# Transposes by DMA, V in batches, corrected GpSimd lengths, rules by unit and 79 packs, in a planned attention and linear-attention kernel

## The chip, the cores, the metric

One core of one Trainium2 chip. The metric is device microseconds (us) of one execution; unless said otherwise a time is the median of several runs. "Span" is the time from the first to the last instruction in the profile; it is 1.7 to 3.1 us shorter than the time of the same run.

## The reference, cut

```python
x = A_x                                   # 1 x 2048 x 512, bf16; 32 heads of 16
g = sigmoid((x * gate_w).sum(-1, keepdims=True))
a = A(x)   # softmax attention: p = softmax(q k^T / 4); o = p v; o @ A_wo
b = B(x)   # linear attention: phi = [softmax(+-q w_phi)], num = phi_q (phi_k^T v), den = phi_q sum(phi_k); (num/den) @ B_wo
return g * a + (1 - g) * b
```

## The kernel before

Nearly all the work is branch A's exponentials: 32 heads of 2048 x 2048 scores. The kernel cuts them into 32 "units" (four heads by 512 queries), each of 16 key tiles by four score tiles of 128 x 512. Most score tiles go TensorE -> PSUM ring -> ScalarE (exp, in calls of three and two tiles) -> TensorE (times V). Some key tiles, the **packs**, skip ScalarE: VectorE and GpSimd build their exponentials arithmetically. Branch B's work fills gaps.

No order is written by hand. The kernel lists operations with an assumed duration, dependencies and a priority, and a **planner** in the kernel plays them through at build time, engine by engine; the order it finds is the order in which each engine gets its instructions. So the assumed durations and the constants decide the program, though no instruction contains them.

```python
PACE = [2.384, 0.458]; RULES = [...]; PIECES = (4, 4)      # constants of the planner, found by search
DVE_COUNT = (1, 3, 2, 1, 2, 3, 1, 2, ...)                  # packs per unit, 76 in all
# a pack (cut): integer scores on VectorE, then split on GpSimd (or VectorE), then a polynomial on VectorE
ws.append(s.op("dve", 0.605, lambda e: e.tensor_scalar(EW[...], self.bk(b), EC, 127 * 65536, ...)))     # x4
fs = [s.op("pool", U * 9.3e-4 + 0.03, lambda e, c=c: e.tensor_scalar(Ef[...], half(0, uint16, c, U), ...),
           alt=U / 1920 + 0.065, port=True) for c in range(US)]      # alt: may run on VectorE instead
hs = [s.op("pool", W * 9.3e-4 + 0.03, lambda e, c=c: e.tensor_scalar(ED[...], half(1, int16, c, W), ...)) ...]
u = s.op("dve", 1.13, Em = Ef * Ef); q = s.op("dve", 0.6, Em = Em * E3 + E1)
g = s.op("dve", 1.13, Em = Ef * Em); v = s.op("dve", 1.13, ED = ED + Em)
# branch B, a query tile (cut): eight transposes on TensorE into a PSUM bank, one copy on VectorE
m = s.op("pe", 0.056, lambda e: e.transpose(pb()[:, P*gg:P*gg+P], self.phi[...], self.iden[:, :]), ...)
ev = s.op("dve", 0.601, lambda e: e.tensor_copy(self.phiT[...], pb()), [m], frees=[b])
# ... and four more transposes and a copy for the result, onT_B
```

Only two PSUM banks (ps_mp) serve pack scores, projections, V, and branch B. An op marked `port` may not overlap a GpSimd op in the plan.

The softmax here doesn't subtract the row's maximum and nothing guards it: scores larger than these inputs give would overflow.

## Time and profile before

| | before |
|---|---|
| time, median of 3 (range) | 858.81 us (857.71 to 859.97) |
| span of the profiled run | 855.9 us |
| ScalarE / VectorE / GpSimd busy | 829.6 / 790.5 / 416.7 us |
| exponential calls; packs | 698; 76 |
| end by the kernel's own planner | 841.8 us |

The prediction below shows the profile's lines. In a group's line, the two numbers after the first bar are the time in which at least one such instruction ran, and the mean duration.

### The profile page before, as it was taken

The page shows a single profiled execution, that of the slowest core. Times are in us where ns is not written, and L with a number is a line of the kernel's source. Part 1 is how long each engine was busy: PE and PEld are TensorE (multiplying, and loading weights), DVE is VectorE, ACT ScalarE, POOL GpSimd, SP SyncE. Part 2 cuts the span into 40 slices and gives each one's busy share as a digit, 9 for nine tenths or more (in the row PEclk, how much of TensorE's full clock was granted, in tenths as well). Part 3 has the DMA queues.
Part 4 walks back from the last instruction along what each step waited for, and adds up shares of the span by engine and source line. Part 5 has one row for each costly group of instructions (what it writes and reads, how often), then busy time and mean ns, then how long its engine had stood idle before and what let it go on. Part 6 is the DMA issues. An engine that isn't in the chain of part 4 may idle for free.

```text
span 855.9 us, 14732 instructions
## 1 busy us (share of the span) xinstructions
PE 792.2 (93%) x5939; PEld 235.5 (28%) x5939; DVE 790.5 (92%) x1178; ACT 829.6 (97%) x770; POOL 416.7 (49%) x548
## 2 busy tenths in 40 slices
PE   8988999999999999999999899999999988898898
PEld 3222233222332223322222222222222222222222
DVE  4899998999879999899999999999999999899995
ACT  6999999999999999999999999999999999899997
POOL 1566043514024466234664754855664366745742
PEclk9999999999999999999999999999999999999999
DMA  6230100000000000000000000000000000000000
GB/s 121 56 76 4 53 4 2 2 5 4 3 2 5 4 5 4 2 4 4 8 12 10 8 17 16 4 4 1 4 5 4 4 4 4 1 4 4 5 20 31
DMA packets 23523, 11.31 MB, mean 13 GB/s; under 512 B 15904, under 2 KB 23456, under 8 KB 23456
## 3 DMA queue, kind: packets, MB, share of 16 engines
q1 hardware_dynamic: 21872, 9.99, 4.4%
q8 instruction: 46, 0.75, 0.4%
q10 hardware_dynamic: 1584, 0.39, 0.2%
q14 instruction: 21, 0.17, 0.1%
HBM read 3.69 MB, written 2.10 MB: 7 GB/s over the span
## 4 chain that ended last, share of the span: by engine, by line
ACT 44%; DVE 40%; PE 7%; POOL 6%; issue 2%; DMA 0%; SPq 0%; POOLq 0%
ACT ET L832 41%; DVE EW L917 9%; DVE Em L936 6%; DVE ED L942 5%; DVE Em L940 5%; POOL ED L931 4%; DVE Em L938 3%; PE ps_ring L815 3%; ACT phi L1086 2%; POOL Ef L927 2%; DVE Ef L927 2%; PE ps_mp L906 1%; DVE fsum L1090 1%; PE ps_ot L860 1%; DVE phi L1092 1%
## 5 line engine op out<-in xcount | busy, mean ns | idle before, releaser
L832 ACT ACTIVATE ET<-ps_ring 128x1536 bf16<-128x1536 f32 (+1 forms) x698 | 800.5, 1302 | 13.3 <-PE ps_ring L815 8.0
L815 PE MATMUL ps_ring<-qT,kT 64*128 64x512 bf16 x1744 | 349.5, 385 | 30.3 <-ACT ET L832 23.6
L927 POOL TENSOR_SCALAR Ef<-EW 128x512 f16<-128x512 uint16 x236 | 165.5, 701 | 301.2 <-DVE EW L917 83.9
L931 POOL TENSOR_SCALAR ED<-EW 128x512 int16<-128x512 int16 x304 | 248.0, 833 | 124.8 <-PE ps_ot L948 34.9
L917 DVE TENSOR_SCALAR EW<-ps_mp 128x512 int32<-128x512 f32 x304 | 196.4, 677 | 13.8 <-PE ps_mp L906 13.0
L860 PE MATMUL ps_ot<-ET,Vaug 128*17 128x512 bf16 x1744 | 169.2, 384 | 2.6 <-DVE T L977 2.3
L815 PEld LDWEIGHTS ps_ring<-qT,kT 64*128 64x128 bf16 x1744 | 73.0, 93 | 235.0 <-ACT ET L832 195.8
L906 PE MATMUL ps_mp<-qT,kT 64*128 64x512 bf16 (+1 forms) x304 | 112.3, 385 | 15.5 <-POOL ED L931 8.2
L936 DVE TENSOR_TENSOR Em<-Ef 128x2048 f16<-128x2048 f16 x76 | 97.5, 1283 | 7.5 <-POOL Ef L927 7.3
L942 DVE TENSOR_TENSOR ED<-ED,Em 128x2048 uint16<-128x2048 int16 x76 | 98.4, 1295 | 2.4 <-POOL ED L931 2.1
L940 DVE TENSOR_TENSOR Em<-Ef,Em 128x2048 f16<-128x2048 f16 x76 | 97.8, 1287 | 0.4
L877 PE MATMUL ps_ot<-zero,iden 128*32 128x512 bf16 (+2 forms) x572 | 96.5, 380 | 0.0
L860 PEld LDWEIGHTS ps_ot<-ET,Vaug 128*17 128x17 bf16 x1744 | 41.2, 87 | 140.4 <-issue 125.0
L938 DVE TENSOR_SCALAR Em<-Em 128x2048 f16<-128x2048 f16 x76 | 61.0, 803 | 0.4
L906 PEld LDWEIGHTS ps_mp<-qT,kT 64*128 64x128 bf16 (+1 forms) x304 | 28.3, 95 | 70.9 <-DVE EW L917 35.0
L1090 DVE TENSOR_REDUCE fsum<-phi 128x64 f32<-128x1024 bf16 x32 | 38.4, 1201 | 4.2 <-ACT phi L1086 4.0
L1092 DVE TENSOR_TENSOR phi<-phi,frec 128x1024 bf16<-128x1024 bf16 x32 | 40.5, 1266 | 0.2
L697 PE MATMUL ps_mp<-Wp,xT 128*128 128x512 bf16 x128 | 40.2, 384 | 0.0
L697 PE MATMUL ps_mp<-xT,WA 128*128 128x512 bf16 x128 | 38.9, 383 | 0.5 <-ACT xT L681 0.5
L1086 ACT ACTIVATE phi<-ps_mp 128x512 bf16<-128x512 f32 x64 | 37.4, 685 | 0.3 <-PE ps_mp L697 0.3
L877 PEld LDWEIGHTS ps_ot<-zero,iden 128*32 128x32 bf16 (+2 forms) x572 | 29.9, 95 | 16.8
L948 PE MATMUL ps_ot<-ED,Vaug 128*17 128x512 bf16 x304 | 29.3, 383 | 4.0 <-DVE ED L942 3.6
(86 smaller groups left out, 460.1 us busy)
## 6 DMA issues: line engine op xcount, KB each, us to landing
qT<-qst SPq DMA_DIRECT2D x120, 16.0 KB, 1.8
out_dram<-outt SPq DMA_DIRECT2D x12, 128.0 KB, 1.7
WA<-in_A_wqkv_dram SPq DMA_DIRECT2D x3, 384.0 KB, 4.5
xr<-in_A_x_dram SPq DMA_DIRECT2D x4, 128.0 KB, 3.2
WBV<-in_B_wqkv_dram SPq DMA_DIRECT2D x1, 512.0 KB, 3.9
WoA<-in_A_wo_dram SPq DMA_DIRECT2D x1, 512.0 KB, 3.8
WoB<-in_B_wo_dram SPq DMA_DIRECT2D x1, 512.0 KB, 4.5
out_dram<-outz SPq DMA_DIRECT2D x4, 128.0 KB, 1.8
```

What stands on the lines that cost most here:

```text
L815: return lambda e: e.matmul(self.ps_ring[:, x % RING, :], self.kT[r, g // 2, kt * P:(kt + 1) * P], self.qT[r, n % 2, i, :], start=True, st ...
L832: self.o_exp.append(s.op("act", w * 0.434 + 0.045, lambda e, b0=b0, s0=s0, w=w: e.activation(self.ET[:, s0:s0 + w, :], self.ps_ring[:, b0: ...
L860: return lambda e: e.matmul(self.ps_ot[32 * i:32 * i + VSL, :], self.Vaug[:, kt, h, :], self.ET[:, (4 * p + k) % NSLOT, :], start=(kt == 0 ...
L877: return lambda e: e.matmul(self.ps_ot[c:c + nc, :], self.iden[r:r + nr, 0:nc], self.zero[r:r + nr, :], start=False, stop=False, tile_posi ...
L906: return lambda e: e.matmul(self.bk(b), self.kT[r, cp, kt * P:(kt + 1) * P], self.qT[r, n % 2, i, :], start=True, stop=True, tile_position ...
L917: ws.append(s.op("dve", 0.605, lambda e, i=i, b=b: e.tensor_scalar(self.EW[:, ew.idx, i * QCH:(i + 1) * QCH], self.bk(b), float(EC), float ...
L927: fs = [s.op("pool", U * 9.3e-4 + 0.03, lambda e, c=c: e.tensor_scalar(self.Ef[:, ef.idx, U * c:U * c + U], half(0, dt.uint16, c, U), floa ...
L931: hs = [s.op("pool", W * 9.3e-4 + 0.03, lambda e, c=c: e.tensor_scalar(self.ED[:, ed.idx, W * c:W * c + W].bitcast(dt.int16), half(1, dt.i ...
L936: u = s.op("dve", 1.13, lambda e: e.tensor_tensor(self.Em[:], Ef(), Ef(), ALU.mult), fs + [self.ed_prev], pr, frees=[ef], port=True)
L938: q = s.op("dve", 0.6, lambda e: e.tensor_scalar(self.Em[:], self.Em[:], E3, E1, op0=ALU.mult, op1=ALU.add), [u], pr, port=True)
L940: g_ = s.op("dve", 1.13, lambda e: e.tensor_tensor(self.Em[:], Ef(), self.Em[:], ALU.mult), [q], pr, frees=[ef], port=True)
L942: vs = [s.op("dve", 1.13, lambda e: e.tensor_tensor(out(), out().bitcast(dt.int16), self.Em[:], ALU.add), [g_] + hs, pr, port=True)]
```

## The change

The intent: take transposes and small copies off TensorE, VectorE and the two PSUM banks; tell the planner longer GpSimd times, nearer to the measured ones; let planner rules differ by unit; and use the room for three more packs. Cut to its core:

```diff
-RULES = [1.148, 0.155, 0.715, 0.527, 2.372]      -PIECES = (4, 4)
+RULES = [0.155, 0.527, 0.1]                      +PIECES = ((2, 2), (2, 4), (4, 4))
+OFF, PRI, SHY, FILL, SLIP, POLY, SHAPE = [33 values each, one per unit] (cut)
-DVE_COUNT = (1, 3, 2, 1, 2, 3, 1, 2, 1, 1, 3, 4, ...)     # 76
+DVE_COUNT = (1, 3, 2, 2, 2, 3, 2, 2, 1, 2, 3, 3, ...)     # 79
-        fs = [s.op("pool", U * 9.3e-4 + 0.03, ...
+        fs = [s.op("pool", U * 8.26e-4 + 0.28, ...        # 512 columns: 0.51 -> 0.70 us
-        hs = [s.op("pool", W * 9.3e-4 + 0.03, ...
+        hs = [s.op("pool", W * 8.26e-4 + 0.165, ...       # 512 columns: 0.51 -> 0.59 us
-        ... 8 x e.transpose(...) on "pe", then tensor_copy to phiT on "dve"
+        ev = s.op("sp", 2.6, lambda e: e.dma_start_transpose(
+            self.phiT[:, pt.idx], self.phi[:, ph.idx].rearrange("p h s f -> p (h s f)")), [o_phi], r + 15,
+            alloc=[pt], frees=[ph], dma=1)
-        ... 4 x e.transpose(...) on "pe", then tensor_copy to onT_B on "dve"
+        self.o_onTB[t] = s.op("sp", 1.3, lambda e: e.dma_start_transpose(
+            self.onT_B[:, bt.idx], self.ob[:, ob.idx, :]), os_, r + 25, alloc=[bt], frees=[ob], dma=1)
+    def emit_V4(self, t, part):       # V of later heads: 16 matmuls for four tiles into one bank, one copy
-                    free = o.run + sum(x[2].run for x in ready[e] ...)     # how far GpSimd may be let in
+                    till = now + o.dur + sum(x[2].dur for x in ready[e] ...)   # ... (cut)
```

"True lengths" below means these two corrected ones. They are true only roughly: an undisturbed piece of 512 columns takes 0.62 us in the trace, the means with waits are 0.70 us (Ef) and 0.83 us (ED) in the kernel before.

More of the change, by code (lines that the diff above doesn't have):

```diff
@@ L31 @@
 LEAD = [16.455462617506317, 8.705434360851719, 19.141216454617272, 18.856826992452106, 21.376333972175523, 40.540151693083416, 4.775252756783429, 10.0]
-PACE = [2.3843439776967976, 0.45802931388055307]
+PACE = [2.413586301706786, 0.45802931388055307]
 BOUNDS = [3.0710501327799653, 8.000889564597248, 7.971137937737645, 16.0, 29.86797202712817]
-RULES = [1.1478886659343592, 0.15539563905827855, 0.7153593749264521, 0.5274031413498357, 2.3718927004339707]
-PIECES = (4, 4)
+RULES = [0.15539563905827855, 0.5274031413498357, 0.1]
@@ L36 @@
+PIECES = ((2, 2), (2, 4), (4, 4))
 CHAIN = 1
 WARM = 3
+OFF = [0.0, 0.0, 0.0, 0.0, 2.691800625687394, -6.716095397832944, 6.540719988102694, 2.7498330404394467, 0.0, 0.0, 0.0, -2.2579236370474356, -2.409484198582825, 0.0, 0.0, 0.0, -0.8759902237228423, 4.467480048248628, 0.0, 0.0, 0.0, 0.0, 0.0, -4.520043988488846, 0.0, 0.0, 0.0, -5.610806173083075, 0.0, -3.9725120228666846, -2.4633716773693948, 0.0, 0.0]
+PRI = [0.0, 1.78558980373506, 0.0, 5.4399768561318895, 0.0, 0.0, -5.515168518014984, 5.2399509275854985, 0.9490998638077267, 0.0, -5.057883055897609, 0.0, -3.218517286352996, 0.0, 4.522122028063479, 0.0, 5.717543899352507, 0.0, -6.495573036306094, 3.531552028337119, 3.576047912456649, 0.0, 0.0, -4.742091436435198, 0.0, 0.0, -9.576418791145084, 7.477283004220624, -1.1952762084850899, -7.9980849912460785, 0.0, 10.423358349149414, 0.0]
@@ new lines @@
+SHY = [0.05939659292837668, 0.5, 0.5, 1.0102736898489502, 0.0, 0.9156313918376744, 0.0, 0.5, 0.29552477015684253, 0.5, 0.5, 0.5, 1.1042928545334503, 0.5, 0.5, 0.5, 0.5, 1.3897029615304355, 0.0, 0.4709512047047394, 0.5, 0.0, 0.5, 0.5, 1.0951553678650432, 0.5, 0.5, 1.3774533903824406, 0.5074017221337324, 0.0, 0.5, 0.10931613263370937, 0.5]
+FILL = [0.5, 0.22374241740231265, 0.5, 0.6175020065897155, 0.5, 0.5735000555490133, 0.024390066267502286, 0.35725811751895753, 0.5, 0.36749487146258475, 0.5, 0.5, 0.5, 0.5, 0.2627895131468908, 0.4237752704298481, 0.5, 0.5, 0.31335957425136196, 0.7480394537915906, 0.5, 0.5, 0.5, 0.5, 0.04128657517781878, 0.5, 0.3615317937946025, 0.554401536243815, 0.5, 0.5, 0.09379059466882533, 0.3404612346283603, 0.5]
@@ new lines @@
+SLIP = [0.0, 0.0, 0.06040700872331797, 0.0, 0.0, 0.0, 0.021168477000203204, 0.0, 0.0, 0.0016465550143923602, 0.0, 0.0, 0.0, 0.0, 0.0, 0.0, 0.0, 0.0, 0.06406254955060428, 0.03531284597062863, 0.0, 0.013902649784111994, 0.0, 0.0, 0.0, 0.0, 0.0, 0.0, 0.0, 0.0, 0.0, 0.01149176932476132, 0.0]
+POLY = [2.3718927004339707, 2.3718927004339707, 2.3718927004339707, 2.3718927004339707, 0.8425927624799181, 2.3718927004339707, 4.282502061990654, 2.3718927004339707, 2.3718927004339707, 2.3718927004339707, 3.8896720368879567, 1.1182564982864798, 2.4545271014588117, 2.3718927004339707, 2.3718927004339707, 2.1427936875512477, -1.3153066215108966, 2.3718927004339707, 2.3718927004339707, 0.5319727150344797, 2.3718927004339707, 2.3718927004339707, 2.3718927004339707, 2.3718927004339707, 2.3718927004339707, 2.3718927004339707, 1.6173863276045077, 2.3718927004339707, -0.2988884624911665, 2.3718927004339707, 5.121320728096021, 2.3718927004339707, 2.3718927004339707]
@@ L38 @@
+SHAPE = [2, 1, 1, 1, 2, 1, 1, 2, 1, 1, 1, 1, 1, 1, 1, 1, 0, 1, 1, 1, 1, 0, 2, 1, 1, 1, 1, 1, 1, 1, 1, 2, 1]
 VSL = 17
@@ L46 @@
 E1, E3 = 61.15205816, 9.99312212
-DVE_COUNT = (1, 3, 2, 1, 2, 3, 1, 2, 1, 1, 3, 4, 1, 2, 2, 3, 3, 3, 3, 2, 3, 2, 2, 4, 1, 3, 3, 3, 3, 2, 4, 3)
+DVE_COUNT = (1, 3, 2, 2, 2, 3, 2, 2, 1, 2, 3, 3, 2, 3, 2, 3, 2, 3, 3, 2, 3, 3, 2, 3, 3, 2, 3, 3, 3, 2, 4, 2)
 def dve_tiles(n):
@@ L80 @@
                  "ready", "seq", "dma", "order", "inc", "tick", "clock", "war", "cols", "lat", "cfg", "exp", "grp", "port",
-                 "gate", "go", "alt", "run", "half")
+                 "gate", "go", "alt", "half", "part")
     def __init__(self, eng, dur, fns, deps, prio, rel, alloc, frees, dma, order, cols=0, cfg="F", port=False,
-                 gate=False, alt=0.0, run=0.0):
+                 gate=False, alt=0.0):
         self.cols = cols
@@ L87, in __init__ @@
         self.half = None
-        self.run = run or dur
         self.port = port or eng == "pool"
@@ L119, in __init__ @@
     def __init__(self):
-        self.SHY, self.REST, self.FILL, self.SAME, self.POLY = RULES
+        self.REST, self.SAME, self.JOIN = RULES
+        self.part = 0
         self.ops = []
@@ L128, in op @@
     def op(self, eng, dur, fns, deps=(), prio=0.0, rel=0.0, alloc=(), frees=(), dma=0, order=(),
-           cols=0, cfg="F", port=False, gate=False, alt=0.0, run=0.0):
+           cols=0, cfg="F", port=False, gate=False, alt=0.0):
         if not isinstance(fns, (list, tuple)):
@@ L133, in op @@
             cols = 90
-        o = Op(eng, dur, list(fns), deps, prio, rel, alloc, frees, dma, order, cols, cfg, port, gate, alt, run)
+        o = Op(eng, dur, list(fns), deps, prio, rel, alloc, frees, dma, order, cols, cfg, port, gate, alt)
         if eng == "dve" and any(getattr(b.pool, "scarce", False) for b in o.frees):
@@ L154, in outlook @@
         q = self.chain[self.at]
+        self.part = q.part
         r, back = now, None
@@ L201, in push @@
             if o.alt:
-                heapq.heappush(future["dve"], (max(when, at(o, "dve") + self.SHY), o.seq, o))
+                heapq.heappush(future["dve"], (max(when, at(o, "dve") + SHY[self.part]), o.seq, o))
         def release(o):
@@ L272, in run @@
                     base = max(0.0, r + (self.TURN if q.cfg != cfg else 0.0) - due)
-                    if late > base + self.SLIP:
+                    if late > base + SLIP[self.part]:
                         held.append(it)
@@ L330, in run @@
                 if parked and not o.port:
-                    free = o.run + sum(x[2].run for x in ready[e] if not x[2].port and x[2].start is None)
-                    free -= max(0.0, hold["pool"] - now)
-                    while parked and free > self.FILL * parked[0].dur:
+                    till = now + o.dur + sum(x[2].dur for x in ready[e] if not x[2].port and x[2].start is None)
+                    for r, _, x in sorted(future[e]):
+                        if r > till + self.JOIN:
+                            break
+                        if not x.port and x.start is None and x is not o:
+                            till = max(till, r) + x.dur
+                    go = max(now + self.TAIL["dve"], hold["pool"])
+                    while parked and till > go + FILL[self.part] * parked[0].dur:
                         c = parked.pop(0)
@@ L338, in run @@
                         heapq.heappush(future["pool"], (now + self.TAIL["dve"], c.seq, c))
-                        free -= c.dur
+                        go += c.dur
                 last = o
@@ L377, in run @@
         return out
-    SLIP = 0.0
     SPARE = 0.26
@@ L646, in consts @@
             fill=1.0, base=0, channel_multiplier=1), [a], prio=-99)
-        self.o_zero = s.op("dve", 0.2, lambda e: e.memset(self.zero[:], 0.0), prio=-300)
+        self.o_zero = s.op("dve", 0.35, lambda e: e.memset(self.zero[:], 0.0), prio=-300)
         self.o_par = s.op("dve", 0.20, lambda e: e.tensor_reduce(
@@ L650, in consts @@
             [self.o_iden], prio=-90)
-        self.o_qz = [s.op("dve", 0.6, lambda e, n=n: e.memset(self.qT[:, n], 0.0), prio=-200 + 101 * n)
+        self.o_qz = [s.op("dve", 0.9, lambda e, n=n: e.memset(self.qT[:, n], 0.0), prio=-200 + 101 * n)
                      for n in range(2)]
@@ L684, in consts @@
         self.o_ot0 = s.op("dve", 0.5, lambda e: e.memset(self.ps_ot[:, :], 1.0), prio=-85)
-        self.o_vones = s.op("pool", 1.0, lambda e: e.memset(self.Vaug[:, :, :, DH:VSL], 1.0), prio=-98,
+        self.o_vones = s.op("pool", 1.87, lambda e: e.memset(self.Vaug[:, :, :, DH:VSL], 1.0), prio=-98,
                              order=[self.o_iden])
@@ L748, in emit_kT @@
             self.kT[:, cp, j * QCH:(j + 1) * QCH], self.bk(b)), 512, dl)
+    def emit_V4(self, t, part):
+        s = self.s
+        t0 = t // 4 * 4
+        n = 8 * DH
+        dl = self.tn(4 * part) + 4 * (t0 + 1) * self.ut - 5.0
+        b = self.bank(1)
+        m = None
+        for x in range(4):
+            for c in range(4):
+                m = s.op("pe", self.c_mm(n), lambda e, x=x, c=c: e.matmul(
+                    self.bk(b)[:, n * x:n * x + n], self.xT[:, c, (t0 + x) * P:(t0 + x + 1) * P],
+                    self.WA[:, c, 2 * D + P * part:2 * D + P * part + n], start=(c == 0), stop=(c == 3)),
+                    [self.d_wv[part]] + self.x_in(t0 // 4) if m is None else (), dl - 1.5, dl - LEAD[5],
+                    alloc=[b] if m is None else (), order=[m], cols=n)
+        o = self.evac(b, m, lambda e: e.tensor_copy(
+            self.Vaug[:, t0:t0 + 4, 8 * part:8 * part + 8, 0:DH],
+            self.bk(b).rearrange("p (t h d) -> p t h d", t=4, d=DH)), 512, dl, [self.o_vones])
+        for x in range(4):
+            self.o_V[(t0 + x, part)] = o
     def emit_V(self, t, part):
+        if part:
+            return self.emit_V4(t, part)
         h0, nh = 8 * part, 8
@@ L821, in main_chain @@
             s.chain.append(o_qk)
+            o_qk.part = units[ua][0]
             if units[ub][1:] == (NT - 1, ORDER[-1]) or ub == len(units) - 1:
@@ L897, in dve_pack @@
         a, z = self.tn(n), self.tn(n + 1)
-        rel = a + (z - a) * (j / nj) - LEAD[0] if n else a + 6
-        pr = rel + LEAD[1]
-        US, HS = PIECES
+        rel = a + (z - a) * (j / nj) - LEAD[0] + OFF[n] if n else a + 6
+        pr = rel + LEAD[1] + PRI[n]
+        US, HS = PIECES[SHAPE[n]]
         ew, ed, ef = Buf(self.EW_p, US + HS), Buf(self.ED_p, 1), Buf(self.Ef_p, 2)
@@ L918, in dve_pack @@
                 self.EW[:, ew.idx, i * QCH:(i + 1) * QCH], self.bk(b), float(EC), float(127 * 65536),
-                op0=ALU.mult, op1=ALU.add), [m], pr if first else -2e3 + pr, frees=[b], run=0.605 * (4 - x)))
+                op0=ALU.mult, op1=ALU.add), [m], pr if first else -2e3 + pr, frees=[b]))
             self.qk_dve[n] = self.eq_prev = m
@@ L926, in dve_pack @@
         gate = (n, j) != (NN - 1, nj - 1)
-        fs = [s.op("pool", U * 9.3e-4 + 0.03, lambda e, c=c: e.tensor_scalar(
+        fs = [s.op("pool", U * 8.26e-4 + 0.28, lambda e, c=c: e.tensor_scalar(
             self.Ef[:, ef.idx, U * c:U * c + U], half(0, dt.uint16, c, U), float(2.0 ** -16), EU,
@@ L930, in dve_pack @@
             alt=U / 1920 + 0.065, port=True) for c in range(US)]
-        hs = [s.op("pool", W * 9.3e-4 + 0.03, lambda e, c=c: e.tensor_scalar(
+        hs = [s.op("pool", W * 8.26e-4 + 0.165, lambda e, c=c: e.tensor_scalar(
             self.ED[:, ed.idx, W * c:W * c + W].bitcast(dt.int16), half(1, dt.int16, c, W), 128.0, float(EM),
@@ L934, in dve_pack @@
             for c in range(HS)]
-        pr += s.POLY
+        pr += POLY[n]
         u = s.op("dve", 1.13, lambda e: e.tensor_tensor(self.Em[:], Ef(), Ef(), ALU.mult), fs + [self.ed_prev], pr,
@@ L951, in pv @@
                 start=False, stop=False, tile_position=(0, 32 * i), skip_group_check=True)
-        return s.op("pe", 0.2155, cfg="C", cols=512, fns=[pv(i) for i in range(4)], deps=vs + [self.o_V[(kt, part)]], prio=pr - s.POLY + LEAD[6], order=[first_pv],
+        return s.op("pe", 0.2155, cfg="C", cols=512, fns=[pv(i) for i in range(4)], deps=vs + [self.o_V[(kt, part)]], prio=pr - POLY[n] + LEAD[6], order=[first_pv],
                     frees=[ed])
@@ L1099, in query_b @@
         ph, o_phi = self.feature(t, 0, r, 1)
-        b = self.bank(1)
         pt = Buf(self.phiT_p, 2)
-        m = None
-        pb = lambda b=b: self.bk(b).bitcast(dt.bfloat16)
-        for gg in range(8):
-            m = s.op("pe", 0.056, lambda e, gg=gg, pb=pb: e.transpose(
-                pb()[:, P * gg:P * gg + P], self.phi[:, ph.idx, 4 * gg:4 * gg + 4].rearrange("p h s f -> p (h s f)"),
-                self.iden[:, :]), [o_phi, self.o_iden], r + 15, alloc=[b, pt] if m is None else (), order=[m],
-                frees=[ph] if gg == 7 else ())
-        ev = s.op("dve", 0.601, lambda e, pb=pb: e.tensor_copy(
-            self.phiT[:, pt.idx].rearrange("p g q -> p (g q)"), pb()), [m], r + 18, frees=[b])
+        ev = s.op("sp", 2.6, lambda e: e.dma_start_transpose(
+            self.phiT[:, pt.idx], self.phi[:, ph.idx].rearrange("p h s f -> p (h s f)")), [o_phi], r + 15,
+            alloc=[pt], frees=[ph], dma=1)
+        ev.lat = 2.8
         ob = Buf(self.ob_p, 1)
@@ L1134, in query_b @@
                 frees=[b]))
-        b = self.bank(1)
-        m = None
         bt = self.b_onTB[t] = Buf(self.onTB_p, 4)
-        pb2 = lambda b=b: self.bk(b).bitcast(dt.bfloat16)
-        for c in range(4):
-            m = s.op("pe", 0.056, lambda e, c=c, pb2=pb2: e.transpose(
-                pb2()[:, P * c:P * c + P], self.ob[:, ob.idx, P * c:P * c + P], self.iden[:, :]), os_, r + 25,
-                alloc=[b, bt] if m is None else (), order=[m], frees=[ob] if c == 3 else ())
-        self.o_onTB[t] = s.op("dve", 0.338, lambda e, pb2=pb2: e.tensor_copy(
-            self.onT_B[:, bt.idx, :, :], pb2()[:, 0:512].rearrange("p (c q) -> p c q", c=4)),
-            [m], r + 27, frees=[b])
+        self.o_onTB[t] = s.op("sp", 1.3, lambda e: e.dma_start_transpose(
+            self.onT_B[:, bt.idx], self.ob[:, ob.idx, :]), os_, r + 25, alloc=[bt], frees=[ob], dma=1)
+        self.o_onTB[t].lat = 2.8
     def outputs(self):
```

## The prediction

> **What bounds the kernel now.** I read the page's busy line first, then its chain, then the groups with shapes kept apart, ScalarE's own waits, and a table of stretches; last the shortest, median and longest durations of lines that share a lock. The page's busy line and the two lines of its chain:
>
> ```profile
> PE 792.2 (93%) x5939; PEld 235.5 (28%) x5939; DVE 790.5 (92%) x1178; ACT 829.6 (97%) x770; POOL 416.7 (49%) x548
> ACT 44%; DVE 40%; PE 7%; POOL 6%; issue 2%; DMA 0%; SPq 0%; POOLq 0%
> ```
>
> ScalarE (ACT) is the fullest engine, but VectorE (DVE) holds almost as much of the chain: two engines bind by turns. ScalarE does the exponentials of three quarters or more of each head's key tiles; the rest, 76 "packs" of 128 keys by 2048 score columns, are exponentials built from arithmetic on VectorE and GpSimd. Moving a pack moves four score tiles from ScalarE to VectorE and GpSimd. The groups, shapes apart (busy us, mean ns; then idle before):
>
> ```profile
> L832 ACT ACTIVATE ET<-ps_ring 128x1536 bf16<-128x1536 f32 x349 | 528.6, 1515 | 10.8 <-PE ps_ring L815 6.1 <-PE ps_ot L860 2.5 <-PE ps_mp L906 0.5
> L832 ACT ACTIVATE ET<-ps_ring 128x1024 bf16<-128x1024 f32 x348 | 379.6, 1091 | 2.5 <-PE ps_ring L815 1.9 <-PE ps_mp L906 0.6
> L757 DVE CAST Vaug<-ps_mp 128x128 bf16<-128x128 f32 x64 | 17.5, 282 | 10.7 <-PE ps_mp L697 10.4
> L1109 DVE COPY phiT<-ps_mp 128x1024 bf16<-128x1024 bf16 x16 | 10.9, 679 | 1.3 <-PE ps_mp L1105 1.3
> L1143 DVE COPY onT_B<-ps_mp 128x512 bf16<-128x512 bf16 x16 | 6.5, 409 | 0.4 <-PE ps_mp L1140 0.4
> ```
>
> The reader sees two things: the exponentials wait for almost nothing (13.3 us in 697 calls), and the copies that the change takes off VectorE are short. The timeline of ScalarE at both ends:
>
> ```profile
> 10.89 19.53 ACT L832 ACTIVATE ET<-ps_ring 128x1536 bf16<-128x1536 f32 x17 [0.91 <-PE ps_ring L815]
> 846.76 1.94 ACT L832 ACTIVATE ET<-ps_ring 128x1536 bf16<-128x1536 f32 x2 [0.52 <-PE ps_ring L815]
> ```
>
> So the exponentials run from 10.89 to 848.70, 837.8 us. ScalarE's busy time in there is 829.6 less 4.4 (table load 1.3, two early copies 1.2, three last output scalings 1.9) = 825.1. Its middle idle is therefore 12.7 us, and that is all that better order could give. The rest is a head of 10.9 and a tail of 7.2 (855.9 - 848.7). Where it idles (stretches; columns PE, PEld, DVE, ACT, POOL busy):
>
> ```profile
> 463.60:499.30 35.70, 32.77 (x234) 9.17 (x234) 34.84 (x51) 34.10 (x32) 19.16 (x28) 1.00 0.04 12
> 677.60:713.20 35.60, 31.65 (x260) 9.34 (x258) 35.11 (x54) 35.02 (x33) 23.45 (x31) 1.00 0.01 3
> 713.20:748.90 35.70, 30.77 (x226) 8.01 (x223) 32.98 (x43) 33.23 (x29) 23.29 (x29) 0.95 0.01 3
> 784.60:820.20 35.60, 30.49 (x221) 8.05 (x220) 32.12 (x40) 33.84 (x30) 27.96 (x34) 1.00 0.01 3
> ```
>
> ScalarE loses 1.6, 0.6, 2.5 and 1.8 us here, mostly where GpSimd is fullest. From the waits:
>
> ```profile
> PE ps_mp L906 <- POOL ED L931: 8.2, 8, 1.6
> PEld ps_mp L906 <- POOL ED L931: 11.5, 10, 1.9
> ```
>
> TensorE, which takes its instructions in order, stands waiting for GpSimd to free a pack's integer buffer, and the next scores for ScalarE stand behind it. Why GpSimd is late shows in shortest/median/longest durations:
>
> ```profile
> L931 POOL TENSOR_SCALAR ED<-EW x304: 613/621/1710, 24.9 to 842.4; 128x512 int16<-128x512 int16 x152
> L927 POOL TENSOR_SCALAR Ef<-EW x236: 620/621/1657, 23.5 to 840.0; 128x512 f16<-128x512 uint16 x118
> L938 DVE TENSOR_SCALAR Em<-Em x76: 631/702/1135, 29.6 to 842.0; 128x2048 f16<-128x2048 f16 x76
> L936 DVE TENSOR_TENSOR Em<-Ef x76: 1154/1220/1649, 27.6 to 840.7; 128x2048 f16<-128x2048 f16 x76
> ```
>
> A GpSimd piece takes 0.62 us, while the kernel's planner places it as 0.51 us (512 x 0.00093 + 0.03 in the code); it then runs into VectorE's next instruction, and one of the two is held up.
>
> **What the Trainium skill says.** "SBUF — State Buffer", section "Who interferes with whom": VectorE's two-port modes, and VectorE instructions with two SBUF inputs against a GpSimd instruction that reads SBUF, exclude GpSimd for a whole instruction. The trace agrees: the same GpSimd piece spreads from 613 to 1710 ns, the same VectorE product from 1154 to 1649. The same section says a DMA never contends with a compute engine, so moved transposes should cost the engines nothing. "ScalarE: Activation LUTs", "What ACT_TABLE_LOAD costs", gives 186 ns + 0.833 ns per column; the trace has 1515 and 1091 ns, a slope of (1515 - 1091) / 512 = 0.828 ns, with the fixed part about 50 ns higher: I use the trace. "DMA: Bandwidth & Descriptors", "DMA Transpose (X-bar)", allows 2-byte data from SP or ACT into SBUF, and only one transposing stream in flight; all transposes here stay on SP. Its sister table in "VectorE: DVE Perf Modes", "The three transpose paths", puts a DMA transpose of 128x128 at 1309 ns. Here a transpose of 128x512 holds the queue 1.26 us and lands 2.7 us after issue (x and weights, from HBM; no SBUF source has run yet).
>
> **The change part by part.** Counts are from the two built programs.
>
> (1) 79 packs for 76: ScalarE has 12 score tiles less, 693 calls for 698. In an undisturbed run of the chain 12 calls take 13.56 us, 1.13 each; a 3-tile and a 2-tile call make 2.26 us per five tiles, 0.452 per tile. 12 x 0.452 = 5.4 us off ScalarE. This lies wholly on the binding path.
>
> (2) Transposes by DMA: off TensorE 128 + 64 transposes (13.0 + 7.5 us busy), off VectorE the two copies, 10.9 + 6.5 = 17.4 us, and 32 uses of the two scarce PSUM banks. None is on ScalarE, so no direct gain. Added to the SP queue: 16 transposes of 128x1024 (estimate 2 x 1.26 = 2.5 us of queue, landed after 4.0) and 16 of 128x512, about 60 us on an idle queue.
>
> (3) V in batches: 48 copies of 0.273 us (17.5 / 64) become 12 of about 0.68 (as the 512-column qst copy, 10.9 / 16): 13.1 - 8.2 = 4.9 us off VectorE, 36 bank uses fewer.
>
> (4) Pack work on VectorE: three packs at 4 x 0.646 (196.4 / 304) + 1.22 + 0.70 + 1.21 + 1.22 (medians) = 6.9 us, together 20.8. The first polynomial step moves towards VectorE: it had 68 pieces of 512 columns (22% of the columns); now 73 of 1024 and 18 of 512 (52%). At a median of 0.415 us for 512 and 0.218 for a 16-column operation of the kind, 1024 columns are an estimate of 0.62 us: 73 x 0.62 + 18 x 0.415 = 52.7, less 68 x 0.415 = 28.2: plus 24.5.
>
> (5) GpSimd: from 540 pieces of 512 to the equal of 468, at 0.62 each 335 to 290 us. It holds the lock less, and the planner now knows its length.
>
> VectorE's sum: waits inside its durations now, (mean - median) x count over the four pack lines, Ef, phi and the normalisation, are 4.8 + 7.7 + 5.5 + 5.5 + 4.4 + 1.6 + 2.4 = 31.9 us. So 790.5 - 31.9 - 17.4 - 4.9 + 20.8 + 24.5 = 781.6 without any such wait; if half stay, about 797. Thus the freed time is spent again, and VectorE stays as full as it was.
>
> (6) ScalarE's middle idle: truer GpSimd lengths and 68 fewer bank uses should shrink it; fuller VectorE and less slack work against. I choose 8 us for 12.7: the waits on GpSimd should mostly go, the small ones remain.
>
> Sum for ScalarE: 10.9 + (825.1 - 5.4) + 8 + 7.2 = 845.8 us of span. The timed median lies 2.9 above the span (858.8 against 855.9): 848.7, rounded to 848.5.
>
> **The rivals.** First, VectorE becomes the bound. For it: it already stands at 98 to 99% in some stretches (35.11 of 35.60 above) and loses no work. Against: 17.4 + 4.9 us leave it, and part of 31.9 us of lock waits. If all lock waits stay it needs about 814 us, packs come late, and ScalarE idles as now or more: 853 to 858. Second, the DMA transposes bite: feature products in TensorE's order wait for a late landing, or heads' query placements queue behind a transpose on SP. Against: both are planned far ahead, landings of 1.7 to 4.3 us are small, and SP mostly waits. If each of 16 query tiles cost 0.5 us, 8 us: about 857. Third, the new order is nearly perfect: middle idle of 2 us gives 842.7; even none gives 840.7, the floor with this many score tiles. Fourth, the transposes hardly matter and the gain is the 5.4 us of the three packs alone: 853.4. All but the worst remain within 2%.
>
> **Range and chances.** 2% faster is below 841.6, which needs middle idle under about one us: 6%. 2% slower is above 876, 27 us over my number, needing a systematic stall: 3%. Range 842.5 to 855.5, from the third rival to the middle of the first.
>
> **What would show it.** Right: about 824 us of ScalarE busy, 693 exponential calls of unchanged durations; middle idle 6 to 10; VectorE near 795 to 805 with its longest pack durations rarer; GpSimd well below 416.7, near 330; TensorE's waits on GpSimd gone; transposes landing in 3 to 5 us with hardly any wait naming them. Wrong: ScalarE's idle before the exponentials at or above today's, named by pack scores or the feature products behind a DMA; GpSimd medians moved; a longer head or tail; or exponential calls themselves slower.

## The result, and the profile after

The changed kernel took **835.47 us** (835.38 to 837.34, four runs) against 859.39 (857.71 to 864.63, four runs). The ratio is 0.9717, 95% interval 0.9673 to 0.9761. A ratio is the mean time of one kernel's runs over that of the other's of the same rounds, so it is not quite the ratio of the two medians. It is 2.8% faster, outside the stated range, and below what the prediction had called the floor (840.7). All outputs are right.

The busy line and the chain that ended last, of the changed kernel:

```profile
PE 765.5 (92%) x5815; PEld 226.2 (27%) x5898; DVE 792.3 (95%) x1157; ACT 819.4 (98%) x765; POOL 298.1 (36%) x399
ACT 96%; PE 2%; DVE 1%; DMA 0%; SPq 0%; issue 0%
```

VectorE is as busy as before, but the chain has left it: 40% there before, 1% now. ScalarE alone decides. Its groups by shape, and its timeline at the two ends:

```profile
L867 ACT ACTIVATE ET<-ps_ring 128x1536 bf16<-128x1536 f32 x346 | 537.5, 1554 | 1.3 <-PE ps_ring L849 0.9 <-PE ps_ot L895 0.3
L867 ACT ACTIVATE ET<-ps_ring 128x1024 bf16<-128x1024 f32 x347 | 391.0, 1127 | 0.0
```

```profile
10.76 19.53 ACT L867 ACTIVATE ET<-ps_ring 128x1536 bf16<-128x1536 f32 x17 [0.91 <-PE ps_ring L849]
809.04 17.02 ACT L867 ACTIVATE ET<-ps_ring 128x1536 bf16<-128x1536 f32 x15
829.02 1.27 ACT L1230 ACTIVATE outz<-ps_mp,gcol 128x512 bf16<-128x512 f32 x2 [2.96 <-PE ps_mp L1189]
```

The exponentials now run from 10.76 to 826.06, 815.3 us, 22.5 less than before. ScalarE's busy time in there is 819.4 - 4.4 = 815.0, so its middle idle fell from 12.7 us to 0.3.

**Busy time hid part of the stall.** The single calls became longer (1515 to 1554 and 1091 to 1127 ns) while the whole became shorter. A call that is queued early starts under its predecessor, and its duration grows by as much: over the well-fed calls of both traces, a nanosecond of earlier start goes with 0.99 to 1.01 ns of longer duration (slopes fitted to starts and durations), while the end comes at the same distance. Before, count times mean less busy is 528.6 + 379.6 - 800.5 = 107.7 us of overlap; after, 537.5 + 391.0 - 791.2 = 137.3, with fewer calls. A call that comes late loses its overlap without showing idle time. The clean measure is from one call's end to the next one's, which I took from the starts and durations in the trace, where an exponential call follows another: a three-tile call ends 1.343 us after its predecessor (median), a two-tile call 0.917, in both kernels. Before, 54 calls were over 15 ns late against that, by 17.66 us together; after, 5 calls, by 0.82 us. So 16.8 us of lateness went, where idle time showed only 12.4. With 12 tiles x 0.452 = 5.4 us that makes 22.2 of the 22.5.

GpSimd and its neighbours, shortest/median/longest durations, after:

```profile
L966 POOL TENSOR_SCALAR ED<-EW x306: 614/620/2012, 23.7 to 821.0; 128x512 int16<-128x512 int16 x148, 128x1024 int16<-128x1024 int16 x5
L962 POOL TENSOR_SCALAR Ef<-EW x85: 620/1047/1927, 24.4 to 817.8; 128x1024 f16<-128x1024 uint16 x67, 128x512 f16<-128x512 uint16 x18
L973 DVE TENSOR_SCALAR Em<-Em x79: 623/682/1256, 27.1 to 820.6; 128x2048 f16<-128x2048 f16 x79
L971 DVE TENSOR_TENSOR Em<-Ef x79: 1157/1214/1677, 25.9 to 819.3; 128x2048 f16<-128x2048 f16 x79
```

The undisturbed durations didn't change; the means did (page and groups: the first polynomial product 1223 ns for 1283 before, the multiply-add 706 for 803, the split ED piece of 512 columns 691 for 833). Collisions became rarer. The plan has a part in it: with the old lengths in the changed kernel (e2) the three means rise again, to 1294, 777 and 763 ns. The lengths alone don't do it: put into the kernel before (e1), they leave them at 1276, 766 and 862 ns. GpSimd also has less to do now (298.1 us busy for 416.7). TensorE's waits on GpSimd, 8.2 and 11.5 us before, are:

```profile
PEld ps_mp L941 <- POOL ED L966: 1.1, 2, 0.6
PE ps_mp L941 <- POOL ED L966: 0.5, 2, 0.3
```

The new operations, from the transposes' own lines (queue time of one in ns, then issue to landing) and the groups:

```profile
L1136 SPq DMA_TRANSPOSE phiT<-phi x16: 1232/1242/2091, 243.3 to 725.2; - x16
DMA to landing us min/median/max: 3.0/3.1/3.5
```

```profile
L1165 SPq DMA_TRANSPOSE onT_B<-ob x16: 1189/1202/1747, 255.8 to 743.8; - x16
DMA to landing us min/median/max: 2.4/2.4/4.0
```

```profile
L962 DVE TENSOR_SCALAR Ef<-EW 128x1024 f16<-128x1024 uint16 x73 | 49.2, 681 | 0.0
L776 DVE CAST Vaug<-ps_mp 128x512 bf16<-128x512 f32 x12 | 8.1, 676 | 1.1 <-PE ps_mp L771 1.1
```

No wait of any engine in the changed kernel's list of waits names a transpose: they are hidden.

### The profile page after: what moved, and what is told of

It is laid out like the page before. It is cut to its first block, busy times and chain, and to the rows that moved or that the text cites. A ratio compares the mean times of both kernels' runs of the same rounds, so it can differ in the third digit from the quotient of the medians.

```text
span 833.6 us, 14440 instructions
## 1 busy us (share of the span) xinstructions
PE 765.5 (92%) x5815; PEld 226.2 (27%) x5898; DVE 792.3 (95%) x1157; ACT 819.4 (98%) x765; POOL 298.1 (36%) x399
## 4 chain that ended last, share of the span: by engine, by line
ACT 96%; PE 2%; DVE 1%; DMA 0%; SPq 0%; issue 0%
ACT ET L867 92%; ACT phi L1121 4%; PE ps_ring L849 1%; DMA xr<-in_A_x_dram 0%; DVE EW L952 0%; PE ps_ring L1189 0%; PE ps_mp L1189 0%; PE ps_ot L895 0%; PE ps_mp L709 0%; SPq L626 0%; DVE wphi L1049 0%; PE ps_ot L983 0%; ACT outz L1230 0%; ACT kT L756 0%; ACT xT L693 0%
## 5 line engine op out<-in xcount | busy, mean ns | idle before, releaser
L867 ACT ACTIVATE ET<-ps_ring 128x1536 bf16<-128x1536 f32 (+1 forms) x693 | 791.2, 1340 | 1.3 <-PE ps_ring L849 0.9
L849 PE MATMUL ps_ring<-qT,kT 64*128 64x512 bf16 x1732 | 343.6, 385 | 53.8 <-ACT ET L867 40.9
L966 POOL TENSOR_SCALAR ED<-EW 128x512 int16<-128x512 int16 (+1 forms) x306 | 211.5, 706 | 401.8 <-DVE Em L975 96.5
L952 DVE TENSOR_SCALAR EW<-ps_mp 128x512 int32<-128x512 f32 x316 | 204.8, 678 | 6.5 <-PE ps_mp L941 4.4
L962 POOL TENSOR_SCALAR Ef<-EW 128x1024 f16<-128x1024 uint16 (+1 forms) x85 | 83.4, 981 | 121.4 <-DVE ED L977 30.3
L912 PE MATMUL ps_ot<-zero,iden 128*32 128x512 bf16 (+2 forms) x716 | 106.0, 378 | 0.3 <-issue 0.2
L941 PE MATMUL ps_mp<-qT,kT 64*128 64x512 bf16 (+1 forms) x285 | 102.0, 380 | 2.8 <-ACT phi L1121 0.8
L971 DVE TENSOR_TENSOR Em<-Ef 128x2048 f16<-128x2048 f16 x79 | 96.6, 1223 | 0.8 <-POOL Ef L962 0.5
L962 DVE TENSOR_SCALAR Ef<-EW 128x1024 f16<-128x1024 uint16 (+1 forms) x91 | 56.5, 630 | 0.1
L912 PEld LDWEIGHTS ps_ot<-zero,iden 128*32 128x32 bf16 (+2 forms) x723 | 35.4, 95 | 24.0
L941 PEld LDWEIGHTS ps_mp<-qT,kT 64*128 64x128 bf16 (+1 forms) x316 | 29.1, 95 | 45.1 <-DVE EW L952 19.5
L709 PE MATMUL ps_mp<-Wp,xT 128*128 128x512 bf16 x109 | 34.8, 384 | 1.0 <-issue 0.6
```

The source lines that it names most:

```text
L849: return lambda e: e.matmul(self.ps_ring[:, x % RING, :], self.kT[r, g // 2, kt * P:(kt + 1) * P], self.qT[r, n % 2, i, :], start=True, st ...
L867: self.o_exp.append(s.op("act", w * 0.434 + 0.045, lambda e, b0=b0, s0=s0, w=w: e.activation(self.ET[:, s0:s0 + w, :], self.ps_ring[:, b0: ...
L912: return lambda e: e.matmul(self.ps_ot[c:c + nc, :], self.iden[r:r + nr, 0:nc], self.zero[r:r + nr, :], start=False, stop=False, tile_posi ...
L941: return lambda e: e.matmul(self.bk(b), self.kT[r, cp, kt * P:(kt + 1) * P], self.qT[r, n % 2, i, :], start=True, stop=True, tile_position ...
L952: ws.append(s.op("dve", 0.605, lambda e, i=i, b=b: e.tensor_scalar(self.EW[:, ew.idx, i * QCH:(i + 1) * QCH], self.bk(b), float(EC), float ...
L962: fs = [s.op("pool", U * 8.26e-4 + 0.28, lambda e, c=c: e.tensor_scalar(self.Ef[:, ef.idx, U * c:U * c + U], half(0, dt.uint16, c, U), flo ...
```

## The experiments

**The theories.** A: the planner before believed GpSimd short, so its plan could not be kept, and the run lost some 14 us against its own plan; with true lengths, constants searched on them give a plan that is kept. B: the transposes and batches free VectorE time and PSUM banks, and that is the gain. C: something else, such as true lengths alone, or the packs alone. Not among the three, but to be watched, is the clock of TensorE, which falls for a few us in some runs ("Plans against spans"). Since each kernel carries its planner, a number is at hand that no profile has: its planned end, to be held against the span. "Searched" below means that I changed the planner's constants at random, some 5,000 plans per search unless said, and kept what lowered the planned end.

### e1: true lengths alone, in the kernel before

```diff
-        fs = [s.op("pool", U * 9.3e-4 + 0.03, ...      -        hs = [s.op("pool", W * 9.3e-4 + 0.03, ...
+        fs = [s.op("pool", U * 8.26e-4 + 0.28, ...     +        hs = [s.op("pool", W * 8.26e-4 + 0.165, ...
```

> The kernel before with the corrected GpSimd lengths in its planner and nothing else. By its own planner the kernel before should end at 841.8 us and ran 855.9 (span), the changed kernel at 833.2 and ran 833.6. Theory A (true lengths make the plan come true; the gain needs a plan re-tuned on true lengths): the planner now writes down 867 us as its end, and the chip keeps to it within about 5 us, so span 862 to 872, slower than before by about 1%, with the waits of TensorE on GpSimd gone. Theory B (transposes and V batches free VectorE and the PSUM banks, and that is the gain): nothing to gain here, 852 to 860. Theory C (true lengths alone are worth the gain): 835 to 845.

868.63 us (ratio 1.0105, 1.0085 to 1.0126), span 865.4 for a planned 867.5: **slower by 1%, as theory A said**: clear of the noise. The plan is now kept, and is a bad one. The chain, and ScalarE's waits:

```profile
ACT 91%; PE 6%; DVE 2%; DMA 0%; issue 0%; SPq 0%; ACTq 0%
```

```profile
ACT ET L832 <- PE ps_ot L860: 23.1, 10, 9.2
ACT ET L832 <- PE ps_ring L815: 0.9, 1, 0.9
```

Ten waits of up to 9.2 us, which the plan itself contains, stand where the kernel before had twenty short ones (8.0 + 2.5 + 1.1 us), most of them not in its plan: run again, the planner shows 4.1 us of ScalarE gaps among the exponentials, against 12.7 measured. Pack scores of TensorE wait for GpSimd only 1.1 us in all. So the old, short lengths did help a plan that had been searched with them. Theory C in its first form falls.

### e2: old lengths in the changed kernel

The reverse edit of e1, in the changed kernel.

> The changed kernel with the old GpSimd lengths (512 columns as 0.51 us) in the planner, all else as in the changed kernel. Planned end 836.5. Theory A: the chip falls behind this plan as it did for the kernel before, by 8 us or more: span 844 to 852, ScalarE's idle before the exponentials back to 8 us or more. Theory B: lengths matter little, 834 to 839.

843.04 us (ratio 0.9812), span 839.6 for a planned 836.5. Neither number was met: the overrun is 3.1 us, less than A's 8, and the span is 6.0 over the changed kernel's 833.6, more than B's. The direction is A's; the size is less than in the kernel before. The changed kernel uses GpSimd much less, which would explain it, but that was not tested by itself. Nor were the constants searched again on the old lengths, so e2 says what wrong lengths cost a plan that was made for true ones (6.0 us), not what a search on old lengths would reach.

### e3: both structures in the kernel before, lengths and constants old

The hunks of the diff for phiT, onT_B and emit_V4, in the kernel before.

> The kernel before with the DMA transposes and the V batches, but its old planner, old lengths, old constants and 76 packs. Planned end 840.9. Theory B: at least half of the gain of 22 us is here, span at or under 845. Theory A: the plan still rests on short GpSimd lengths and is overrun by 8 us or more: 849 to 857.

862.59 us (ratio 1.0037, 1.0011 to 1.0062), span 859.1 for a planned 840.9: **nothing gained, and the plan overrun by 18 us**, an estimated 3 us of it with falls of the clock ("Plans against spans"). Theory B in its simple form falls. The chain, and TensorE's waits on GpSimd:

```profile
DVE 44%; ACT 38%; PE 9%; POOL 5%; issue 3%; DMA 0%; POOLq 0%
```

```profile
PEld ps_mp L928 <- POOL ED L953: 10.7, 10, 2.2
PE ps_mp L928 <- POOL ED L953: 5.4, 6, 1.7
```

This is the kernel before's picture: freed time is no use while the order is wrong.

### e4: the old structure, true lengths, searched afresh

```diff
 # changed kernel, but: transposes on TensorE, V tile by tile, 76 packs
-OFF, PRI, SHY, FILL, SLIP, POLY, SHAPE, LEAD, BOUNDS, RULES, DVE_COUNT = (as changed)
+OFF, PRI, ... = (searched; cut)
```

> The structure of the kernel before (transposes on TensorE with copies on VectorE, V tile by tile, 76 packs) under the changed planner with true lengths, its constants by unit searched afresh by me for some 5,500 plans. Planned end 844.9. Theory A: the chip keeps the plan within 3 us: span 843 to 848, so more than 8 us of the gain come with neither transposes nor batches nor packs. Theory B: no gain, 853 or more.

849.32 us (ratio 0.9879, 0.986 to 0.9899), span 845.3 for a planned 844.9. **10.6 us of the 22.3 us of span come with neither transposes nor batches nor packs**: true lengths, the changed planner, and constants searched on them. These three were not separated: the changed planner with old lengths and an equal search was not run, so that the longer search is a part, or even most, of the 10.6 us stays possible.

### e5 to e8: what each structure is worth, at equal search

One starting point (all by-unit constants set back to one value each), 79 packs, one budget of search, four structures: all parts; transposes on TensorE; V tile by tile; neither.

```diff
-OFF = [0.0, 0.0, 0.0, 0.0, 2.69, ...]   (and six more lists)
+OFF = [0.0] * 33; PRI = [0.0] * 33; SHY = [1.148] * 33; FILL = [0.715] * 33; ...   then searched (cut)
```

> Control for the searching. The changed kernel with all its parts and 79 packs, but the constants by unit set back to one value each (planned end 856.8) and then searched afresh by me with a fixed budget of about 5,000 plans. Planned end 840.9. If the chip keeps an honest plan, span 839 to 844. Then some 7 us of the change's 22 are only the longer search behind its constants, since every part of it is in here. If the parts themselves carry the gain, whatever the constants, 832 to 836.

> As the control (flat start, same budget, 79 packs, V batches), but the transposes back on TensorE with their copies on VectorE and their PSUM banks. Planned end 838.4, which is under the control's 840.9. Theory A (plans decide): span 837 to 842, so the DMA transposes are worth nothing that this search can resolve. Theory B (they free 17.4 us of VectorE and 32 bank uses that were needed): slower than the control by 5 us or more, 846 to 852.

> As the control (flat start, same budget, 79 packs, DMA transposes), but V tile by tile. Planned end 842.4. Theory A: 841 to 846, 1 to 2 us from the control. If the batches matter much: 848 or more.

> As the control (flat start, same budget, 79 packs), but with neither DMA transposes nor V batches. Planned end 847.9. If VectorE and bank room is needed for 79 packs, this is the slowest of the four: 847 to 852, some 7 us over the control, though each part undone alone costs 0 to 2. If structure is worthless at equal search, 839 to 844.

| run | median us | span | planned end |
|---|---|---|---|
| e5 all parts | 848.82 | 846.5 | 840.9 |
| e6 transposes on TensorE | 841.16 | 838.6 | 838.4 |
| e7 V tile by tile | 843.51 | 841.6 | 842.4 |
| e8 neither | 851.56 | 850.2 | 847.9 |

Three plans were kept within 2.5 us, e5 was not. In e8 the clock of TensorE fell once, and its one run without a fall had a span of 847.7 us, just as planned. In e5 the granted clock of TensorE fell for two short times. The line is from the windows view of e5; its columns are the stretch, its length, the busy times of TensorE, its weight loads, VectorE, ScalarE and GpSimd (number of instructions in parentheses), then the granted clock, the DMA engines' busy share and the GB/s:

```profile
315.00:325.00 10.00, 8.58 (x53) 2.45 (x53) 7.44 (x14) 7.62 (x7) 2.48 (x4) 0.66 0.08 18
```

ScalarE was busy 7.62 of 10 us there. A second such stretch (640 to 656, clock 0.79) cost ScalarE 1.8 us. Apart from this, the control says that searching is itself worth some 7 us: e5 has every part of the change and was planned 7.7 us worse. With by-unit constants this search is too noisy to rank single parts: the structure with one part less even came out best.

### e9 to e12: the same four, one set of rules for all units

Far fewer constants, which the same budget was meant to search better. It did for all parts and for V tile by tile (planned ends 5.2 and 3.6 us earlier than in e5 and e7), not for the other two (4.8 and 4.7 us later than in e6 and e8).

```diff
+OFF = PRI = [0.0] * 33; SHY = [0.0] * 33; FILL = [0.368] * 33; SLIP = [0.0579] * 33; POLY = [3.92] * 33; SHAPE = [0] * 33
+LEAD = [15.98, 8.74, 17.68, 26.17, 23.23, 30.86, -0.69, 20.16]      # e9; e10 to e12 searched likewise
```

> All parts of the change, 79 packs, true lengths, but one set of rule constants for all units instead of one per unit (no per-unit offsets and priorities), searched by me with about 5,500 plans. Planned end 835.7, against 833.2 for the changed kernel. If rules by unit matter little, span 835 to 839, 2 to 5 us over the changed kernel's 833.6. If they carry the gain, 842 or more.

> As the run before it (one set of rules, same budget), transposes back on TensorE. Planned end 843.2 (another search from the same start ended at 847.2). If the room that DMA transposes make is what lets 79 packs fit, span 842 to 847, 6 to 10 over the run with all parts. If not, within 3 us of it.

> As e9, V tile by tile. Planned end 838.8: span 838 to 842, so the V batches are worth about 3 us; if they are worth nothing, within 1 us of e9.

> As e9, neither DMA transposes nor V batches, 79 packs. Planned end 852.6. If VectorE room is the limit: 851 to 856, with its idle before the exponentials near 20 us, and slower than the 76-pack run of the old structure (845.3): three packs more than VectorE has room for cost time. If structure doesn't matter, 836 to 842.

| run | median us | span | planned end |
|---|---|---|---|
| e9 all parts | 837.35 | 836.3 | 835.7 |
| e10 transposes on TensorE | 845.78 | 844.6 | 843.2 |
| e11 V tile by tile | 839.08 | 837.4 | 838.8 |
| e12 neither | 854.74 | 852.3 | 852.6 |

All four came out as planned within 1.5 us. Two things follow. Rules by unit, with the longer search behind them, are worth 2.7 us here (836.3 against 833.6), 3.6 against e14 below. And **structure does matter once the plan is right**: neither against both costs 16.0 us, against 3.2 us the other way in e3. The size depends on the search: e8 against e5 gives 3.7 us, with e5's falls of the clock in it; the better search of each structure gives 13.9 (850.2 against 836.3). By the same rule one structure alone comes within 1.1 us (e11) or 2.3 us (e6) of both: either one makes most of the room. ScalarE's waits in e12:

```profile
ACT phi L1119 <- PE ps_mp L709: 10.2, 3, 7.1
ACT ET L865 <- PE ps_ot L893: 6.5, 4, 3.5
ACT ET L865 <- PE ps_ring L847: 2.1, 3, 0.9
```

These name results that sit in the two scarce PSUM banks (ps_mp) and the accumulators that close a unit (ps_ot): packs and projections come too late. e12 is also 7.0 us slower than e4, which has the same structure and 76 packs, and e8 4.9 us: without the room, three more packs seem to cost time, though differences between searches are as large. What each structure is worth alone stays open within some 6 us: transposes on TensorE ran at 838.6 in one search and 844.6 in the other.

### e13: 76 packs with all other parts

```diff
+DVE_COUNT = (76 packs); constants searched (cut)
```

> The change with all parts but 76 packs as before, true lengths, searched. Planned end 837.8 with ScalarE's idle between exponentials at 0.1 us. If three packs are worth just ScalarE's 12 tiles (5.4 us, since ScalarE has no other wait left): span 838 to 840, 4 to 6 over the changed kernel. If the packs cost VectorE more than they give: 833 or less.

841.86 us (ratio 0.9796), span 840.3 for a planned 837.8. This is 0.3 us above the range expected. ScalarE was busy 824.6 us, 5.2 more than with 79 packs: the 5.4 of the prediction. Its remaining waits:

```profile
ACT ET L867 <- PE ps_ring L849: 2.6, 3, 1.1
```

The plan had none of these, and they are not the packs' doing: all three (at 291.5, 293.9 and 370.4 us, 2.2 us of lateness together) stand at the run's two falls of the TensorE clock, from 288.6 and 367.1 us, 3.4 us each at 0.50. Against the changed kernel on the same chip (e16) the packs gave 840.3 - 834.8 = 5.5 us; without that lateness it would be some 3.3 (an estimate, 5.5 - 2.2; but e16 began its exponentials 0.9 us later than e13), and the two plans are 4.6 apart.

### e14 to e16: is there more?

> The changed kernel, same parts and 79 packs, its constants searched further by me. Planned end 832.5, 0.6 under the changed kernel's plan. ScalarE has only some 1 us of waits left there, so at most 1 us can be had: span 832.5 to 833.5, if the plan is kept.

> 80 packs, searched. Planned end 834.0: the last exponential ends 1.5 us earlier than in the changed kernel, but the added pack sits in the last unit and lengthens the tail. If the plan is kept, 833.5 to 836; ScalarE busy 1.8 us less than the changed kernel's 819.4. If VectorE is full, 837 or more.

> The changed kernel itself again, to be compared with the two searched further on the same chip: 833 to 836 of span.

On one chip: the changed kernel again 836.26 us (835.59 to 837.60), its constants searched further (18,000 plans) **834.81 us** (834.49 to 835.17; ratio to the kernel before 0.9713), 80 packs 837.09 us. The kernel searched further beats the other two, by 1.4 us or more in the median: small, but the ranges don't meet. 80 packs end their exponentials sooner, yet lose it in the tail, because the added pack stands in the last unit: the wait before the last output scaling is longer than the changed kernel's 2.96.

```profile
ACT outz L1230 <- PE ps_mp L1189: 5.5, 1, 5.5
```

### e17: the plain undo

Transposes back on TensorE in the changed kernel, all constants kept.

> The changed kernel with the transposes put back on TensorE and nothing else touched: its constants stay those that were searched with DMA transposes. Planned end 854.6. Read plainly this would say that the DMA transposes are worth 21 us, nearly the whole gain; with constants searched afresh the same structure ran at 838.6 and at 844.6. Expected span 852 to 858 if the chip keeps the plan; 836 to 846 if the constants' fit to the structure doesn't matter.

858.83 us (ratio 1.0002), span 857.1 for a planned 854.6. Read alone, this would say that the DMA transposes are the whole gain. The same structure with constants searched for it ran at 838.6 and 844.6. So a plain undo measures here mostly the fit of the constants: 12 us or more of the 23.5. ScalarE waits 19.5 us for the accumulators:

```profile
ACT ET L867 <- PE ps_ot L895: 19.5, 11, 5.0
```

### Plans against spans

| kernels | span less planned end, us |
|---|---|
| old GpSimd lengths: before, e3, e2 | +14.1, +18.2, +3.1 |
| true lengths, no fall of the clock: changed, e1, e4, e6, e7, e9, e14, e15, e16 | +0.4, -2.1, +0.4, +0.2, -0.8, +0.6, +0.2, +1.0, +1.6 |
| true lengths, one fall: e8, e10, e11, e12, e17 | +2.3, +1.4, -1.4, -0.3, +2.5 |
| true lengths, two falls: e5, e13 | +5.6, +2.5 |

A fall is a stretch of 3.4 or 6.8 us in which the granted clock of TensorE stood at 0.50 (those in the last 12 us of a span are left out). The kernel before and e2 had one, e3 three. A run with a lower mean clock is longer: over 34 runs of the kernel before, the mean span is 855.9 us at a clock of 0.998 (seven runs) and 864.0 at 0.982 (two), about 0.5 us per 0.001, so that a fall of 3.4 us goes with about 1 us (an estimate from these). By this estimate that is 1 us of the 14.1 and 3 of the 18.2, and most of the overrun of e5, e8, e13 and e17; the overrun with old lengths stands. A fall can also be a stall's effect: in the kernel before ScalarE waited 1.4 us at 741.9 us and the clock fell at 742.5. The eight runs of the changed kernel, e16's with them, all had a clock of 1.000; the runs of the kernel before mostly 0.992 to 0.998, so an estimated 1 to 4 us of the 23.9 us in the medians goes with the clock.

## Why the prediction was wrong

The step that failed is **(6), ScalarE's middle idle**, with the sum built on it. It chose 8 us for 12.7, and 0.3 came: 7.7 us. And its base was wrong: "all that better order could give" took busy time (825.1 less 5.4) as work. It came out as 815.0, 4.7 less, since lateness also hides inside busy time. Those two make 12.4 of the 13.2 us between 848.7 and 835.5; the rest is the offset between span and timed median (2.9 taken, 1.9 came) less 0.2 at the two ends. The 2.9 set the median of three runs against the span of another, quicker one, which itself took 857.95 us.

Why 8 was too much: the prediction saw the cause (0.62 us run, 0.51 planned) but treated it as one wait of several to be reduced. It was the reason why the plan as a whole could not be kept (e1: with true lengths alone the overrun goes from 14.1 to -2.1 us), and a plan searched on true lengths, with all parts, is nearly free of waits and is kept (0.3 us of idle in the changed kernel). How much of that the lengths, the planner and the search each gave is open (e4). One reading was loose too: of its four stretches the one that lost most, 2.5 us, holds the run's fall of the clock, not the fullest GpSimd. The planned end was in reach as a comparison and would have shown the 14 us.

Step by step:

- (1) Twelve tiles, 5.4 us: right. e13 shows 5.2 us of busy time; its 5.5 us of span have about 2 us from falls of the clock in them, and the plans differ by 4.6.
- (2) Transposes off the engines: right that none waits for them and that the gain is not direct. Wrong in size: 2.5 us of queue and 4.0 to landing were expected for 128x1024, 1.24 and 3.1 were measured. What it missed is their worth as room: at 79 packs and equal search, both structures together are 16.0 us in one search (e12 against e9) and 3.7 in the other, 13.9 by the better of each, in late packs and projections and not in ScalarE's own work.
- (3) V batches: 12 copies of 0.676 us, 8.1 together, as worked out.
- (4) The first polynomial step on VectorE: 0.68 us for 1024 columns instead of 0.62; 49.2 + 7.3 = 56.5 us against 52.7.
- (5) GpSimd: 298.1 us busy, near 330 was said.
- VectorE's sum: 797 was said, 792.3 came. Half of the 31.9 us of waits inside durations was kept in the sum; from the same lines ((mean - median) x count, over the four pack lines and phi) about 9 stayed.
- Rivals: the first is refuted for this structure (VectorE at 95%, 1% of the chain). Without the structures (e12) packs do come late, as it said, yet VectorE, at 806.7 us of 852.3, holds only 6% of the chain. The second didn't occur. The third, a nearly perfect order, is what came, only that its floor of 840.7 stood 4.7 us too high. The fourth, packs alone, is about 5 of 24.

One path through the 22.3 us of span, in this order: true lengths and search in the old structure 10.6 (before to e4), both structures at 76 packs 5.0 (e4 to e13), three packs and the longer search 6.7 (e13 to the changed kernel; about 2 us of this is e13's falls of the clock). Another order divides it differently, as e3 and e12 show; the parts are not additive.

## What to carry to other kernels

Where a planner decides the order, hold its planned end against the measured span before anything else: a gap says that an assumed duration is wrong or, as in e5 and e13, that the clock fell, and closing it comes before every structural idea. Judge a part of such a kernel only after searching the constants again for the kernel without it, at the same budget; a plain undo measures the fit. And take an engine's lost time from the end of one call to the end of the next, not from its idle time: late calls lose their overlap inside "busy".

## What the Trainium skill lacked or had wrong

- "ScalarE: Activation LUTs", "What ACT_TABLE_LOAD costs", gives an overlap of about 93 ns between back-to-back calls. Here a well-fed three-tile and a two-tile call last 1554 and 1127 ns by the trace and end 1.343 and 0.917 us after their predecessors, an overlap of about 210 ns each. After idle a call lasts 1451 and 1024 ns (medians of 32 and 3 calls, kernel before), a fixed part of 170 ns over a slope of (1451 - 1024) / 512 = 0.834: the 50 ns that the prediction found above the page's 186 are overlap. And no page says that an ACTIVATE's duration grows when it is queued earlier (1515 to 1554 ns), so that lateness hides in busy time: 16.8 us of lateness went, 12.4 us of idle.
- "VectorE: DVE Perf Modes", "The three transpose paths", gives 1309 ns for one DMA transpose of 128x128. From SBUF to SBUF, eight blocks in one transfer held the queue 1.24 us and landed after 3.1, four blocks 1.20 and 2.4: the queue time hardly grows with the blocks (0.04 us for four more), the landing does (0.7 us). The page has one block only and no growth.
- "GPSIMD Engine Reference", section "Elementwise — side-by-side cycle accounting", gives no fixed cost for a one-input piece. Here 512 columns take 0.620 us and 1024 take 1.047: (1047 - 620) / 512 = 0.83 ns per column and about 0.19 us fixed.
- "TensorE: Matmul & The Clock Gate", section "HAM oscillation — how this bites in real kernels", puts the halved clock down to idle gaps of TensorE of over about 3.4 us. The halving is seen here (14 falls to 0.50 in ten of the traces), such gaps are not: the longest in the 6.8 us before a fall was 1.9 us. What the records show is a low load: in the 3.4 us before a fall TensorE was busy 43 to 63% in twelve of the fourteen (52% in the kernel before, 61 and 43% in e5; the other two are e10 with 77 and e8 with 100%). The next section of that page, "A second HAM failure mode: psum-queue depth-cycling", does tell of falls from short, frequent idles, but gives no load. The records can lack some matmuls, and what sets a fall off was not tested.
